# Later raw weights, one queue for the holes, and another order of block 0 in a fused RWKV-6 and tanh-shrink kernel

## The chip, the cores and the metric

One core of a Trainium2 chip runs the whole program in one launch. The metric is the device time of an execution in microseconds (us); runs are compared by their median.

## The reference, cut to what matters

Attention with a decaying state per head, for 4 batches, 8 heads, 768 tokens and 48 channels; then a dense block over 3072 tokens, 384 in, 2048 hidden, 384 out.

```python
for t in range(S):
    cur = np.einsum('bhd,bhe->bhde', u[None] * kt, vt)
    y[:, :, t] = np.einsum('bhd,bhde->bhe', rt, state + cur)
    state = wt[:, :, :, None] * state + np.einsum('bhd,bhe->bhde', kt, vt)
...
h = x @ w_in            # x: y as (3072, 384)
g = h - np.tanh(h)
return (g @ w_out).astype(np.float32)
```

## The kernel before

The work is cut into 8 blocks of 384 tokens (4 batches, two halves each). A block has an attention part and a dense part. While the dense part of block i runs, over 16 steps f of 128 hidden columns each, the attention of block i+1 is prepared between its steps. Block 0 has nobody before it: its attention is done by `boot`, alone, in two halves (pairs of heads 2 and 3, then 0 and 1).

**Attention.** Chunks of 64 tokens. `behind` (a scan on VectorE, L417) makes the decays behind each token, `take_whole` (L437) the whole decay of a chunk, `times_behind` (L431) multiplies k by them; `before` (L404, L405) and `times_before` (L424) do the same for r, into the tile `pre`. `own` and `earlier` are score products on TensorE (`gram`, L480), written through a mask by VectorE (L487). `turn` transposes k on TensorE (L502) and ScalarE copies it (L508). `update_half` (boot, L601) and `update_1` (L560) make the state products; the states are scans on VectorE in the boot (L616) and eleven small operations (L572) in block 0. `result` sums products with states (`from_states`, L662) and with scores (`from_scores`, L680); `result_out` (L714) copies the sum to the tiles `xT`. Rows for which there is no room go through the tile `late`, and `fill_holes` (L721) carries them by six small transfers of 24 KB into the holes of `xT`. In block 0 the term of a token with itself is made by `product_u`, `product_r`, `product_sum` (L370, L374, L378) from tokens loaded in another layout, and put in by `diagonal_in` (L385); the r tokens are loaded into the tile that `times_before` reads.

**Dense part.** Step f: `first` (L826) makes h on TensorE in a PSUM bank and ScalarE copies it out (L829). VectorE takes its square s (L855), ScalarE makes qa from s (L858), VectorE makes h times s and then g (twice L832). `Second.add` (L903) multiplies g with w_out, three steps later in block 0. Later blocks use a form with fewer products (L950). In block 0, h of step 0 and 3 onward goes to the bank `hp`, h of steps 1 and 2 to the first two banks of the sums, which `Second.add` needs after them.

**Weights.** They arrive as raw 64-bit words in 16 units of 768 KB (`more_weights`, L250), five buffers, in the order of `UNITS`. ScalarE converts a unit in three pieces (L263), VectorE joins them (L267). Three units are loaded and converted in the boot and right after; the others in block 0, so many pieces after step f as `PIECES` says.

**Order.** The instructions of TensorE, VectorE, ScalarE and SyncE (SP) stand in their queues in the order in which the program issues them; only GpSimd's (POOL) order is left to a scheduler. An engine waits at the head of its queue. `begin_behind(ins, dma)` makes a load wait until an instruction has ended; SP then holds everything behind it. `busy(to, n)` (L303) issues n products that nobody reads, beside the work. In `plan(0)`, `phases`, `before`, `ahead` and `loads` say behind which step f of block 0 a part of block 1 (or 2) is issued. `bound` (L448) is a sum on ScalarE that checks that no decay is over 1.

Of the kernel before, what the change touches and what calls it, by code (L numbers as in the profile page):

```python
# [52 lines left out]
L = 64  # L53
# [19 lines left out]
RAWS = 5  # L73
LAG = 2
LAST = 5
PIECES = 2, 1, 2, 3, 3, 3, 3, 3, 3, 3, 4, 4, 4
UNITS = [(0, 0), (0, 1)] + [u for j in range(NF // 2 - 2) for u in ((1, j), (0, j + 2))] + [(1, NF // 2 - 2),
                                                                                      (1, NF // 2 - 1)]
LATE = 3
# [46 lines left out]
def kernel(  # L126
# [181 lines left out]
    class Block:  # L308
# [153 lines left out]
        def gram(self, ps, lhs, rhs, p0, n, m=None, ahead=0, late=0):  # L462
            width = L // 2 if m else L
            ps_t = scratch(ps)
            busy(ps_t[:, 0], ahead)
            if late:
                busy(ps_t[:, 0], late, later_ident)
            used = ps_t[:, :, 0:n * NCP * width]
            gr = used.rearrange("s h (p c t) -> s h p c t", p=n, c=NCP)
            for p in range(p0, p0 + n):  # L470
                for c in range(NCP):
                    for h in range(2):
                        for par in range(2):
                            rows = slice(64 * h, 64 * h + D)
                            src = self.chunk(rhs, p, 2 * c + par, rhs == "pre" and not m)[rows]
                            dst = gr[64 * par:64 * par + 64, h, p - p0, c, :]
                            if m:
                                src = src.rearrange("d (b two m) -> d b two m", two=2, m=m)[:, :, 1, :]
                                dst = dst.rearrange("s (b m) -> s b m", m=m)
                            self.done = nc.tensor.matmul(dst, lhsT=self.chunk(lhs, p, 2 * c + par)[rows], rhs=src,  # L480
                                                         start=True, stop=True)
            return used

        def masked(self, ps, lhs, rhs, mask, p0, **fill):
# [102 lines left out]
        def update_half(self, pair, p0):  # L587

            self.by_column = [t[:, 0:D * NCH].rearrange("d (e c) -> d e c", c=NCH) for t in pair]
            for x in range(UP):  # L590
                if x:
                    nc.tensor.drain().then_inc(fence, 1)
                    fences.append(None)
                    nc.tensor.wait_ge(fence, len(fences))
                for c in range(0, NCH, 2):
                    for h in range(2):
                        for par in range(2):
                            p = (x + par) % UP
                            toks = slice(64 * par, 64 * par + 64)
                            e0 = (p0 + p) * D2 + h * D  # L600
                            nc.tensor.matmul(self.by_column[p][64 * h:64 * h + 64, :, (c + par + 1) % NCH],  # L601
                                             lhsT=self.ks[toks, p0 + p, c // 2, 64 * h:64 * h + 64],
                                             rhs=self.v[toks, c // 2, e0:e0 + D], start=True, stop=True)

# [64 lines left out]
        def from_scores(self, yp, slots, first, last):  # L669
            for n, slot in slots:  # L670
                for p in reversed(slot):
                    for c in range(NCP):
                        for h in range(2):
                            for par in range(2):
                                toks = slice(64 * par, 64 * par + 64)
                                e0 = 64 * (h ^ (p % 2))
                                f0 = p * D2 + h * D
                                n0 = (n * NCP + c) * L
                                wide = L if self.halved and p == KC - 1 else D
                                nc.tensor.matmul(yp[p % 2][e0:e0 + wide, par, n0:n0 + L],  # L680
                                                 lhsT=self.v[toks, c, f0:f0 + wide],
                                                 rhs=A[toks, h, p, c, :],
                                                 start=(first and n == slots[0][0] and c == 0),
                                                 stop=(last and (n, c) == (slots[-1][0], NCP - 1)),
                                                 skip_group_check=True)

        def results(self, ps, halved=False):
            self.width = D if halved or isinstance(ps, Kept) else L
# [315 lines left out]
    def plan(i):  # L1004
# [1 line left out]

        formed_w = {}
        if i == 0:
            phases = {5: ("turn",), 6: ("update",), 10: ("earlier",), 13: ("result 1",)}
            before = {0: ("behind 2", "take_whole 2"), 1: ("behind 0", "take_whole 0"), 2: ("times_behind 2",),  # L1010
                      3: ("times_behind 0",), 4: ("before 2",), 5: ("before 0",), 6: ("product_u", "bound 2"),
                      7: ("held", "bound 0"), 8: ("times_before",), 10: ("product_r",),
                      11: ("product_sum",), 12: ("diagonal_in 2", "diagonal_in 0")}
            ahead = {15: ("behind 2", "take_whole 2")}
            loads = {f: "weights" for f in (0, 1, 3, 4, 5, 6, 7, 8, 9, 10)}
# [51 lines left out]
    def run(ops):  # L1067
        for op in ops:
            op()
# [13 lines left out]
    def boot(ps, pair, blk, later):  # L1083
# [3 lines left out]
            blk.load(name, p0, n)  # L1087
        blk.load_v(h1, UP)
        blk.load("k", h2, UP)
        more_weights(nc.sync)  # L1090
        blk.load_v(h2, UP)
        blk.load("r", h2, UP)

# [10 lines left out]
        blk.turn_1(ps, h1)  # L1104
        blk.times_before(h1, UP)
        earlier = blk.earlier(ps, h1)
        begin_behind(blk.done, more_weights(nc.sync))
        blk.behind(h2, UP)
        blk.take_whole(h2, UP)
        first_a, first_b = convert(*raws.pop(0))  # L1110
        own()
        blk.turn_2(h1)
        run(first_a[:2])
        blk.update_half(pair, h1)
        blk.times_behind(h2, UP)
        blk.times_u(h2, UP)
        blk.turn_1(ps, h2)
        blk.turn_2(h2)
        earlier()
        run(first_a[2:])  # L1120
        blk.totals_by_column(h2)
        blk.results(ps, halved=True)
        blk.result("from_scores", both[0])
        run(blk.states_half(h1))
        blk.result("from_states", both[0], True)
        begin_behind(blk.opened, more_weights(nc.sync))
        blk.before(h2, UP)
        own = blk.own(ps, h2)
        blk.update_half(pair, h2)
        blk.times_before(h2, UP)  # L1130
        blk.result_out((3,), nc.scalar.copy)
        blk.result_out((2,))
        earlier = blk.earlier(ps, h2, ahead=2)
        blk.fill_holes([nc.sync, nc.gpsimd])
        begin_behind(blk.done, later.load("w"))
        more_weights(nc.sync)
        second_a, second_b = convert(*raws.pop(0))
        third_a, third_b = convert(*raws.pop(0))
        run(second_a)
        own()  # L1140
        onwards = blk.states_half(h2)
        blk.results(ps, halved=True)
        busy(blk.yp[0][:, 0], 4)
        blk.result("from_states", both[1])
        earlier(1, 1)
        earlier(0, 1)
        begin_behind(third_a[0](), more_weights(nc.sync))
        run(third_a[1:2])
        more_weights(nc.sync)
        later.load("k")  # L1150
        for p in reversed(both[1]):
            blk.result("from_scores", (p,), True, more=True)
        run(onwards)
        run(first_b)
        blk.result_out((1,), nc.scalar.copy)
        blk.result_out((0,), nc.vector.tensor_copy)
        run(third_a[2:])
        run(second_b)
        run(third_b)
        blk.held(0, NPAIR)  # L1160

    mains, pieces = ExitStack(), []
    ps_a = Kept(mains.enter_context(tc.tile_pool(name="ps_a", bufs=1, space=PSUM)))
    ps_h = mains.enter_context(tc.tile_pool(name="ps_h", bufs=1, space=PSUM))
    hp, *acc = [ps_h.tile([P, BANK], F32, name=name, tag=name) for name in ("hp", "acc0")]
    xT = blocks[0].begin()
    with tc.tile_pool(name="ps_boot", bufs=1, space=PSUM) as ps_boot:
        boot(Turns([scratch(ps_boot)] + ps_a.both), [hp] + acc, blocks[0], blocks[1])
# [24 lines left out]
    for i, blk in enumerate(blocks):  # L1193
# [8 lines left out]
        second = Second(row0, acc, few[i]) if few[i] < NF else None  # L1202
        for f in range(NF):
            now = i * NF + f
            for op in ahead_of_h:
                op()
            h, made = first(here, f, ([hp, *acc][f] if now in (1, 2) else hp)[:, 0:NB])
            g, ahead_of_h, square, later_ops = slight(h, now, i, f)
            some = ({4: (0, 2), 6: (2, 4), 8: (4, 6), 9: (6, 8), 14: (8, len(SUMS))} if later else
                    {4: (0, 4), 6: (4, 8), 8: (8, len(SUMS))}).get(f) if summed else None  # L1210
# [178 lines left out]
```

## Time and profile before

| what | value |
|---|---|
| median of 3 runs | 555.12 us (554.82 to 555.69) |
| the profiled execution | 555.16 us, its span 553.3 us |
| TensorE products, weight loads | busy 536.6 and 400.7 us |
| VectorE, ScalarE, GpSimd | busy 460.3, 404.3, 5.2 us |
| raw weights | 16 loads of 768 KB, median 5.3 us from issue to landing |
| HBM read, written | 44.73 MB, 4.72 MB |

PE is TensorE's products, PEld its weight loads, DVE is VectorE, ACT ScalarE, SPq the queue of SyncE. A row of a timeline has the start, the duration (of all that were merged), engine, line, operation, out<-in, shape and count, and in brackets the idle time before it with what ended it; "issue" means that the engine waited for nothing the profile shows. In a table of stretches the columns are the stretch, its length, the busy time of PE, PEld, DVE, ACT and POOL, the granted clock of TensorE, the busy share of the transfer engines and GB/s. A row of the queues has number of pieces, megabytes and share. L12 is line 12 of the kernel.

### The profile page before, as it was taken

To read this page: it belongs to the slowest core of one execution; us is meant where nothing else is said; L and a number is where in the kernel's file an instruction comes from. 1 tells how busy PE (TensorE), PEld (TensorE's weight loads), DVE (VectorE), ACT (ScalarE), POOL (GpSimd) and SP (SyncE) were. 2 spreads that over 40 slices of the span, in tenths; PEclk is the share of its full clock that TensorE was granted. 3 is DMA by queue.
4 is the path that set the end of the run, shared out by engine and by line. 5 is a ranking of instruction groups with operands and counts; after the bars stand their busy time and mean duration, and the time that the engine had idled before them with its cause. 6 is when DMAs were issued, how large, how long until landed. Compare 5 with 4: busy or idle time off the path is not lost.

```text
span 553.3 us, 13985 instructions
## 1 busy us (share of the span) xinstructions
PE 536.6 (97%) x5645; PEld 400.7 (72%) x5645; DVE 460.3 (83%) x942; ACT 404.3 (73%) x815; POOL 5.2 (1%) x33
## 2 busy tenths in 40 slices
PE   6789999999999999999999999999999999999996
PEld 3546566678777787778778787777878787787873
DVE  7699989999988899789797799979797897557563
ACT  5689897797667886588766886588865885666561
POOL 1100000000000000000000000000000000000000
PEclk9899999999999999999999999999999999999999
DMA  8598454243302642135211732136232420100101
GB/s 279 186 391 313 155 191 126 85 117 88 117 12 85 104 117 90 64 88 142 90 55 44 144 117 64 50 87 158 60 97 58 91 54 4 56 0 1 43 2 46
DMA packets 53445, 56.29 MB, mean 102 GB/s; under 512 B 21504, under 2 KB 51328, under 8 KB 53376
## 3 DMA queue, kind: packets, MB, share of 16 engines
q1 hardware_dynamic: 52992, 55.18, 33.9%
q8 instruction: 45, 0.74, 0.5%
q14 instruction: 24, 0.20, 0.1%
q10 hardware_dynamic: 288, 0.10, 0.1%
q0 software_dynamic: 96, 0.07, 0.0%
HBM read 44.73 MB, written 4.72 MB: 89 GB/s over the span
## 4 chain that ended last, share of the span: by engine, by line
PE 90%; ACT 2%; DVE 2%; issue 0%; PEld 0%; PEldq 0%; DVEq 0%
PE hp L826 43%; PE acc L950 26%; PE att L950 6%; PE acc L903 4%; PE att L680 2%; PE att L480 2%; PE att L662 2%; PE acc L928 2%; PE att L560 2%; ACT up L263 1%; DVE w_sb L267 0%; ACT h L829 0%; DVE s L855 0%; ACT qa L858 0%; DVE post L417 0%
## 5 line engine op out<-in xcount | busy, mean ns | idle before, releaser
L826 PE MATMUL hp<-xT,w_sb 128*128 128x384 f32 x756 | 265.9, 488 | 2.0 <-ACT h L829 1.9
L826 PEld LDWEIGHTS hp<-xT,w_sb 128*128 128x128 f32 x756 | 135.1, 190 | 74.6 <-ACT h L829 3.2
L829 ACT ACTIVATE h<-hp 128x384 f32<-128x384 f32 x126 | 61.6, 489 | 101.2 <-PE hp L826 101.1
L950 PE MATMUL acc<-forms,g 128*128 128x128 f32 x954 | 133.6, 276 | 0.5
L950 PEld LDWEIGHTS acc<-forms,g 128*128 128x128 f32 x954 | 121.6, 192 | 10.2 <-issue 1.2
L832 DVE SCALAR_TENSOR_TENSOR h<-h,s 128x384 f32<-128x384 f32 x128 | 70.7, 552 | 51.7 <-ACT s L847 51.6
L873 DVE TENSOR_TENSOR g<-g 128x256 f32<-128x256 f32 x265 | 103.4, 420 | 8.0 <-PE acc L950 7.2
L848 ACT ACTIVATE qa<-s,shift 128x384 f32<-128x384 f32 x113 | 69.6, 616 | 3.7
L850 ACT ACTIVATE junk<-s,shift 128x384 bf16<-128x384 f32 x113 | 67.7, 600 | 0.0
L832 DVE SCALAR_TENSOR_TENSOR g<-qa,h 128x384 f32<-128x384 f32 x112 | 61.7, 551 | 1.7 <-ACT qa L858 0.2
L847 ACT ACTIVATE s<-h 128x384 f32<-128x384 f32 x113 | 59.1, 523 | 3.6
L950 PEld LDWEIGHTS acc<-w_sb,g 128*128 128x128 f32 x318 | 46.7, 191 | 9.7 <-ACT sums L918 0.3
L950 PE MATMUL acc<-w_sb,g 128*128 128x128 f32 x318 | 53.1, 276 | 0.1
L950 PE MATMUL att<-w_sb,g 128*128 128x128 f32 x212 | 35.5, 275 | 0.0
L950 PEld LDWEIGHTS att<-w_sb,g 128*128 128x128 f32 x212 | 31.1, 192 | 5.3
L903 PE MATMUL acc<-w_sb,sums 128*128 128x384 f32 x96 | 34.1, 490 | 0.4 <-ACT h L829 0.3
L985 DVE TENSOR_TENSOR sums<-sums 128x256 f32<-128x256 f32 x84 | 33.0, 408 | 1.7 <-ACT sums L962 1.4
L263 ACT ACTIVATE up<-raw 128x768 f16<-128x768 f32 (+1 forms) x32 | 32.3, 1061 | 0.0
L903 PEld LDWEIGHTS acc<-w_sb,sums 128*128 128x128 f32 x96 | 17.8, 190 | 12.7 <-ACT h L829 0.9
L405 DVE TENSOR_TENSOR_SCAN pre<-w,start 128x780 f32<-128x780 f32 x14 | 25.0, 1783 | 0.5
L417 DVE TENSOR_TENSOR_SCAN post<-w,seed 128x780 f32<-128x780 f32 x14 | 24.9, 1776 | 0.0
L850 ACT ACTIVATION_READ_ACCUMULATOR junk<-s,shift 128x1 f32 x113 | 21.1, 187 | 0.0
(110 smaller groups left out, 513.4 us busy)
## 6 DMA issues: line engine op xcount, KB each, us to landing
raw<-in_weights SPq DMA_DIRECT2D x16, 768.0 KB, 5.3
w<-in_wT SPq DMA_DIRECT2D x7, 780.0 KB, 4.5
k<-in_kT SPq DMA_DIRECT2D x7, 768.0 KB, 4.7
r<-in_rT SPq DMA_DIRECT2D x7, 768.0 KB, 4.5
v_sb<-in_v SPq DMA_DIRECT2D x7, 576.0 KB, 4.0
k<-in_tokens SPq DMA_DIRECT2D x7, 576.0 KB, 3.9
r<-in_tokens SPq DMA_DIRECT2D x7, 576.0 KB, 5.2
out_y<-sums SPq DMA_DIRECT2D x18, 128.0 KB, 1.9
```

What stands on the lines that cost most here:

```text
L263: return lambda: nc.scalar.activation(out=to, in_=of, func=AF.Copy, scale=scale, bias=bias)
L405: return nc.vector.tensor_tensor_scan(out=self.tile("pre")[:, cols], data0=self.tile("w")[:, cols], data1=start[:, 0:n * NCH * LP], initia ...
L826: nc.tensor.matmul(hp, lhsT=w_in_sb[:, f, kc, :], rhs=xT[kc], start=(kc == KC - 1), stop=(kc == 0))
L829: return h, nc.scalar.activation(out=h, in_=hp, func=AF.Copy, scale=1.0 / UPSCALE)
L832: return lambda: nc.vector.scalar_tensor_tensor(out=out, in0=in0, scalar=scalar, in1=in1, op0=op0, op1=ALU.mult)
L847: nc.scalar.activation(out=s, in_=h, func=AF.Square)
L848: nc.scalar.activation(out=qa, in_=s, func=AF.Square, bias=shift[:, 4:5])
L850: nc.scalar.activation(out=junk[:, 0:NB], in_=s, func=AF.Relu, bias=shift[:, 5:6], accum_out=excess[:, at:at + 1])
L873: return lambda: nc.vector.tensor_tensor(out=G[:, to:to + 2], in0=two(G, g_at(q, a0), g_at(q, a1)), in1=two(G, g_at(q, b0), g_at(q, b1)), ...
L903: nc.tensor.matmul(acc, lhsT=g[:, j * P:(j + 1) * P], rhs=w_out_sb[:, f, :], start=(f == self.first), stop=(f == NF - 1))
L950: nc.tensor.matmul(to, lhsT=G[:, g_at(q, a), :], rhs=rhs, start=start, stop=stop, skip_group_check=True)
L985: ops.append(lambda op=op, at=at: nc.vector.tensor_tensor(out=at[0], in0=at[1], in1=at[2], op=OPS[op]))
```

## The change

- Raw weights of the boot: none is issued among the first loads. The first waits for the first product of `earlier` of half 1, the second for the last product of `from_scores` of half 1, the third for the last product of `update_half` of half 2; then `w` of block 1, a fourth without a gate, a fifth behind the second unit's last piece, k, and a sixth. The conversions move with them: in the boot two units whole and two pieces of the third (before: three units).
- Holes of the boot: all six transfers are issued by POOL (before: three by SP, three by POOL). One `busy` more, 5 for 4.
- `totals_by_column` of half 2 is issued earlier on ScalarE.
- Block 0: ScalarE's copy of h of a step stands ahead of qa of the step before (before: behind it). h of step 4 goes to a bank of `ps_a` instead of `hp`. Of the pieces of conversion, one follows step 0, three step 1, none the next two calls, then 2, 4, 3 and so on.
- Attention of block 1: `behind 2` with `take_whole 2` moves to the end of the boot; `behind 0` from step 1 to step 2; `times_behind`, `before`, `product_u`, `held`, `times_before`, `turn`, `update` each one step later; `bound` of block 1 from steps 6 and 7 to 9 and 10. `product_r`, `earlier` and what follows keep their steps.
- `bound` of block 0 moves from steps 13 and 14 of block 0 to steps 1 and 6 of block 1.

```diff
-PIECES = 2, 1, 2, 3, 3, 3, 3, 3, 3, 3, 4, 4, 4
+PIECES = 0, 0, 2, 4, 3, 3, 3, 3, 3, 3, 4, 4, 4
...
         if i == 0:
-            phases = {5: ("turn",), 6: ("update",), 10: ("earlier",), 13: ("result 1",)}
-            before = {0: ("behind 2", "take_whole 2"), 1: ("behind 0", "take_whole 0"), 2: ("times_behind 2",),
-                      3: ("times_behind 0",), 4: ("before 2",), 5: ("before 0",), 6: ("product_u", "bound 2"),
-                      7: ("held", "bound 0"), 8: ("times_before",), 10: ("product_r",),
+            phases = {6: ("turn",), 7: ("update",), 10: ("earlier",), 13: ("result 1",)}
+            before = {2: ("behind 0", "take_whole 0"), 3: ("times_behind 2",), 4: ("times_behind 0",),
+                      5: ("before 2",), 6: ("before 0",), 7: ("product_u",), 8: ("held",),
+                      9: ("times_before", "bound 2"), 10: ("product_r", "bound 0"),
                       11: ("product_sum",), 12: ("diagonal_in 2", "diagonal_in 0")}
...
         blk.load("k", h2, UP)
-        more_weights(nc.sync)
         blk.load_v(h2, UP)
...
-        begin_behind(blk.done, more_weights(nc.sync))
+        begin_behind(blk.opened, more_weights(nc.sync))
...
         blk.turn_2(h1)
-        run(first_a[:2])
+        blk.totals_by_column(h2)
         blk.update_half(pair, h1)
...
         earlier()
-        run(first_a[2:])
-        blk.totals_by_column(h2)
+        run(first_a[:2])
         blk.results(ps, halved=True)
         blk.result("from_scores", both[0])
+        begin_behind(blk.done, more_weights(nc.sync))
         run(blk.states_half(h1))
         blk.result("from_states", both[0], True)
-        begin_behind(blk.opened, more_weights(nc.sync))
...
         blk.update_half(pair, h2)
+        updated = blk.done
...
         earlier = blk.earlier(ps, h2, ahead=2)
-        blk.fill_holes([nc.sync, nc.gpsimd])
+        run(first_a[2:])
+        blk.fill_holes([nc.gpsimd])
+        begin_behind(updated, more_weights(nc.sync))
         begin_behind(blk.done, later.load("w"))
         more_weights(nc.sync)
...
-        run(second_a)
+        run(second_a[:2])
+        begin_behind(second_a[2](), more_weights(nc.sync))
...
-        busy(blk.yp[0][:, 0], 4)
+        busy(blk.yp[0][:, 0], 5)
...
-        begin_behind(third_a[0](), more_weights(nc.sync))
-        run(third_a[1:2])
+        later.load("k")
         more_weights(nc.sync)
-        later.load("k")
...
-        run(third_a[2:])
+        run(third_a[:2])
         run(second_b)
-        run(third_b)
+        later.prepare("behind 2")
+        later.prepare("take_whole 2")
         blk.held(0, NPAIR)
-
-    mains, pieces = ExitStack(), []
+        return [(third_a[2], third_b)]
...
-            for op in ahead_of_h:
+            for op in ahead_of_h if i else ():
                 op()
-            h, made = first(here, f, ([hp, *acc][f] if now in (1, 2) else hp)[:, 0:NB])
+            to = [hp, acc[0], acc[1], hp, ps_a.both[0][:, 0]][now] if now < 5 else hp
+            h, made = first(here, f, to[:, 0:NB])
+            for op in ahead_of_h if not i else ():
+                op()
...
-                ops = square + behind
+                ops = square + converting(pieces, 1)
             elif now == 1:
-                ops = rest + converting(pieces, 1) + square + formed + behind
+                ops = rest + square + converting(pieces, 3)
...
-            if i == 0 and f in (NF - 3, NF - 2):
-                blk.bound(HALVES[f - NF + 3])
-            if i == 0 and f == NF - 2:
+            if i == 1 and f in (1, 6):
+                blocks[0].bound(HALVES[f // 6])
+            if i == 1 and f == 6:
                 nc.gpsimd.memset(states[0][:, :, 0, 0:D], 0.0)
```

The rest of the diff keeps, in `gram`, `update_half` and `from_scores`, the first or the last product, for the gates.

More of the change, by code (lines that the diff above doesn't have):

```diff
@@ L464, in gram @@
             ps_t = scratch(ps)
+            self.opened = None
             busy(ps_t[:, 0], ahead)
@@ L481, in gram @@
                                                          start=True, stop=True)
+                            self.opened = self.opened or self.done
             return used
@@ L600, in update_half @@
                             e0 = (p0 + p) * D2 + h * D
-                            nc.tensor.matmul(self.by_column[p][64 * h:64 * h + 64, :, (c + par + 1) % NCH],
+                            self.done = nc.tensor.matmul(self.by_column[p][64 * h:64 * h + 64, :, (c + par + 1) % NCH],
                                              lhsT=self.ks[toks, p0 + p, c // 2, 64 * h:64 * h + 64],
@@ L679, in from_scores @@
                                 wide = L if self.halved and p == KC - 1 else D
[L680 to L685, printed above, removed]
+                                self.done = nc.tensor.matmul(yp[p % 2][e0:e0 + wide, par, n0:n0 + L],
+                                                             lhsT=self.v[toks, c, f0:f0 + wide],
+                                                             rhs=A[toks, h, p, c, :],
+                                                             start=(first and n == slots[0][0] and c == 0),
+                                                             stop=(last and (n, c) == (slots[-1][0], NCP - 1)),
+                                                             skip_group_check=True)
         def results(self, ps, halved=False):
@@ L1156, in boot @@
         blk.result_out((0,), nc.vector.tensor_copy)
-        run(third_a[2:])
+        run(third_a[:2])
         run(second_b)
-        run(third_b)
+        later.prepare("behind 2")
+        later.prepare("take_whole 2")
         blk.held(0, NPAIR)
-    mains, pieces = ExitStack(), []
+        return [(third_a[2], third_b)]
+    mains = ExitStack()
     ps_a = Kept(mains.enter_context(tc.tile_pool(name="ps_a", bufs=1, space=PSUM)))
@@ L1167 @@
     with tc.tile_pool(name="ps_boot", bufs=1, space=PSUM) as ps_boot:
-        boot(Turns([scratch(ps_boot)] + ps_a.both), [hp] + acc, blocks[0], blocks[1])
+        pieces = boot(Turns([scratch(ps_boot)] + ps_a.both), [hp] + acc, blocks[0], blocks[1])
     ps_d = mains.enter_context(tc.tile_pool(name="ps_d", bufs=1, space=PSUM))
```

## The prediction

> **What bounds the kernel now.** First the page: who is busy, at which clock, and what fetches code.
>
> ```profile
> PE 536.6 (97%) x5645; PEld 400.7 (72%) x5645; DVE 460.3 (83%) x942; ACT 404.3 (73%) x815; POOL 5.2 (1%) x33
> ...
> q8 instruction: 45, 0.74, 0.5%
> ```
>
> TensorE bounds the whole; only its idle time and its half-clock time can be won. Queue 8 is TensorE's code: 0.74 MB in 45 pieces is 16.4 KB each, and 11,290 loads and products over 45 is about 250 instructions a piece.
>
> Second, TensorE's waits up to 100 us and its timeline in the boot and at the `earlier` scores of block 1, with the DMA view of 19.4 to 19.6 and SP's timeline:
>
> ```profile
> PE hp L826 <- ACT h L829: 1.9, 1, 1.9
> ...
> 16.26 0.84 PE L662 MATMUL att<-pre,first_states 48*48 48x64 f32 x29 [0.55 <-issue]
> ...
> 21.70 0.25 PE L601 MATMUL acc<-v_sb,ks 64*64 64x48 f32 x1 [2.75 <-issue]
> ...
> q8 instruction: 1, 0.02, 29.2%
> ...
> 12.19 4.65 SPq L250 DMA_DIRECT2D raw<-in_weights  x2
> ```
>
> In the boot TensorE twice waits for nothing but "issue": until 16.26 and, for 2.75 us in the middle of `update_half`, until 21.70. I read both as waits for code: between the two resumes lie 126 loads, 126 products and 3 others, 255 instructions, one piece. A piece is asked for when the one before it is entered: the piece that ends the second wait was asked for at 16.26, and its transfer is the one at 19.40. It took 0.93, and TensorE resumed 1.36 later. Raw weights were issued at 16.50 (the second of the x2, ending at 16.84, 0.34 long), so the code waited 3.14 us behind them. The next piece, asked for at 21.70 with no raws under way, started after 1.12.
>
> Third, the engines in stretches, at the boot's end and in block 0:
>
> ```profile
> 23.00:24.00 1.00, 1.00 (x34) 0.61 (x23) 0.94 (x2) 0.62 (x1) 0.13 (x2) 0.60 0.00 0
> 24.00:25.00 1.00, 1.00 (x4) 0.17 (x2) 1.00 (x5) 0.00 (x0) 0.00 (x0) 0.50 0.37 42
> ...
> 40.00:46.00 6.00, 5.48 (x17) 3.34 (x18) 5.79 (x11) 6.00 (x10) 0.00 (x0) 1.00 0.92 336
> 46.00:52.00 6.00, 6.00 (x50) 3.84 (x52) 5.80 (x11) 6.00 (x10) 0.00 (x0) 1.00 0.92 321
> ```
>
> The column before the last two is the granted clock: 0.60, 0.50, 0.50, 0.70 in the four us from 23 is 3.4 us at half, after 3.4 us in which TensorE had run only 1.5. And VectorE (the third pair) works 5.8 of 6 us here: from 28 to 66 us it is as full as TensorE. What it must do before TensorE may go on decides. That place is here:
>
> ```profile
> 65.64 1.75 DVE L424 TENSOR_TENSOR pre<-r,pre 128x1536 f32<-128x1536 f32 x1
> ...
> 66.80 2.20 PE L826 MATMUL hp<-xT,w_sb 128*128 128x384 f32 x6
> ...
> 67.42 0.38 SPq L366 DMA_DIRECT2D r<-in_tokens  x1
> ...
> 68.94 1.63 PE L480 MATMUL att<-pre,post 48*64 48x64 f32 x96
> ...
> 73.66 1.36 DVE L374 TENSOR_TENSOR k<-k,r 128x1152 f32<-128x1152 f32 x1 [1.26 <-DMA r<-in_tokens]
> ```
>
> `times_before` (L424) ends at 67.39; the scores that need it (L480) start when their queue reaches them, at 68.94: VectorE is 1.5 us ahead. After 66.8 TensorE never waits again.
>
> **The change, part by part.** The sum is made against the profiled execution, 555.16 us (span 553.3), 0.04 over the median of 555.12.
>
> *Raws later.* No transfer is added; their places change. The first is now gated by the first product of `earlier` (11.2, so issued about 11.3), before the code piece asked for at 11.56 and so ahead of it; 11.3+2.9 (16.50 to 19.40) +0.93+1.36 gives 16.5 instead of 16.26. The second is gated by the last L680 (14.23+0.90) and issued at 15.2, 1.3 earlier than the raws of 16.50 before; the code behind it starts at 15.2+2.9=18.1 and TensorE resumes at 18.1+0.93+1.36=20.4 instead of 21.70. Then: rest of `update_half` 0.34, two fills 0.48 (7 took 1.68), L480 0.9, five fills 1.2 (one more than before, on the path: 0.24), L662 0.95, the fence 0.45 (as in the first half), L680 0.9: the L714 copies start at 25.6, at full clock, where they started at 28.02. Bounds: the next piece is asked for at 20.4 and the third raws are issued 0.40 later. Raws issued 0.24 after a request (16.26) held it up, those issued 0.63 after (11.56, 12.19) did not. If held, it starts at 20.8+2.9, TensorE resumes at 26.0 where it would be at 24.9, and the 2.4 us shrink to 1.3. I take 1.8, the middle, since 0.40 lies between the two rows.
>
> The Trainium skill (DMA: Bandwidth & Descriptors, Queues, rings and completion order) says an engine finishes a whole packet of descriptors of one queue before it turns to another; the 3.14 us agree.
>
> *Holes in POOL's queue alone.* Six issues at 0.52 (three took 1.57) from about 18.9 (18.31 before, plus the first raws landing later) end at 22.0; the last lands 3.1 later, at 25.1. The third part of the first L826 needs it at 26.9. Cost nothing, under 1.8 us of cover; SP's loads (w, raws) no longer stand behind them, but w waits for its own gate, L480.
>
> *h ahead of qa, and other banks.* The 1.9 us before L826 (waiting for h(3) behind a qa) and 0.8 us before L903 (for h(2)) go. They are worth nothing by themselves if VectorE is what TensorE meets next.
>
> *Scans and turn later.* From the end of VectorE's L714 copies on, its list up to L424 holds one step of the dense part more: L267, two L832, one L855, which take 67.31 to 69.82, 2.51 us. In the list the scan and its small op (1.92) stand before s(0), so s(0) ends 3.37 after the copies; then qa(0) 0.53 and three conversions on ScalarE (0.81+0.94+0.94) end at 6.6, while VectorE reaches their L267 at 5.9: a new wait of 0.8. One more for qa(7), 0.3. So L424 ends at 67.39+2.51+0.8+0.3-1.8=69.2, and L480 starts at 69.25 instead of 68.94: **+0.3**. The boot's gain is spent. TensorE arrives about 2.8 us earlier: it waits there. If the scan finds w late, this grows: w is issued at 22.2 behind 2 us of raws and took 4.7, so lands near 27; the scan is due at 29.14+0.87-1.8=28.2; cover 1 us.
>
> *r tokens.* Their load waits for L424; before, two dense steps and 1.26 of waiting lay between L424 and L374, now one. With the 6.2 us of before (67.42 to 73.6), L374 stays 6.2 behind L424, and the diagonal (L385, ended 84.94) comes at 84.94+3.6-1.8=86.75, against a slot for L680 at 86.10+0.3: +0.35. With the k tokens' 3.9 us nothing. The page's median for r tokens is 5.2: I take **+0.2**.
>
> *Bounds of w in block 1.* Two of 1.1 us on ScalarE, which waits for TensorE there (4.26 busy of 6 at 94 to 100). Nothing; a stall there would cost at most 2.2.
>
> *Clock.* A wait of 2.8 us fits into one 3.4 us stretch. The boot's stretch with 1.5 busy was followed by half clock; the wait before L826 left 1.6 busy in some 3.4 us and was not. With 0.6 to 1.9 busy, by phase, half clock follows in about three phases of five. It costs 3.4/2=1.7 if all dense; small products lose little (L662 32 in 0.72 at half, 22 in 0.42 at full, 17%), so with L480's 1.6 us inside it is 0.3+0.9=1.2. Bounds 0 and 1.7; I take **1.1**, near the second.
>
> The Trainium skill (TensorE: Matmul & The Clock Gate, Part 1) puts the drop after an idle window of about 3.4 us, free-running. By that a 2.8 us wait is harmless and the sum is 0.5; the trace had a drop after a window that was 44% busy, and the measurement decides.
>
> Sum: 0.3+0.2+1.1=+1.6: **556.8 us**.
>
> **The rivals.**
> - *No half clock*: the wait at L480 falls across two stretches. 555.7. Chance 0.25.
> - *Faster: the code passes the raws.* If the second piece starts 1.12 after its request, as at 21.70, TensorE resumes at 16.5+1.12+2.29=19.9, or 19.0 where the first piece is in time too; the copies come 2.9 to 3.8 us early, L480 at 68.2 to 67.2, 0.8 to 1.7 gained, with the clock kept. 553.9. Deciding point: the request must reach its engine before the raws of 15.2; the 16.26 row, lost with a lead of 0.24, speaks against. Chance 0.20.
> - *The third raws hold up the third piece*: 1.3 early instead of 1.8 and half clock, or in the boot once more: 557.5 to 558. Chance 0.12.
> - *The stall is no fetch* and stays at 21.70: only the boot's half clock is won, the copies come 1.1 early: 556.8+0.7=557.5. The Trainium skill (Runtime: NRT & Kernel Launch, Instruction fetch mechanics) calls fetching mostly hidden; 255 instructions between two resumes speak against it here. Chance 0.07.
>
> **The numbers.** 0.36 for the forecast. Faster by over 0.2% (1.1 us, about what a measurement of this kernel can tell): the second rival, 0.20. Slower: forecast, third, fourth, less a part near the bound: 0.53. Same: 0.27. Low 553.9 is the faster rival; high 558.0 the third.
>
> **What would show it.** After: an "issue" gap in `update_half` that ends near 20.4; L714 near 26; full clock at 24; then a wait of about 2.8 us of TensorE before the L480 of block 1 for L424, and half clock behind it. Wrong, if that wait is under 1 us, or L714 starts before 24.5.

## The result, and the profile after

The changed kernel takes 559.84 us (median of 7 runs, 557.3 to 561.71); the kernel before, run beside it on the same chip, takes 555.69 (554.59 to 555.98). The ratio is 1.0078, with a 95% interval of 1.0057 to 1.0099: slower by 0.8%. The profiled execution took 559.87 us (span 558.1), 4.71 more than the profiled execution before. Lines after L464 stand a few lines further down now: L480 is L481, L601 is L603, L662 is L664, L680 is L682, L714 is L716, L826 is L828, L903 is L905.

The page, its first line of busy time:

```profile
PE 540.1 (97%) x5646; PEld 403.4 (72%) x5646; DVE 460.5 (83%) x942; ACT 404.2 (72%) x815; POOL 6.7 (1%) x36
```

TensorE has one product more (the fifth fill, a product of `busy` that nobody reads) and is busy 3.5 us longer: nearly the same work ran longer at half clock. TensorE's waits up to 110 us, and its timeline in the boot:

```profile
PE att L481 <- DVE pre L424: 3.3, 1, 3.3
PE acc L603 <- issue: 3.0, 1, 3.0
...
PE hp L828 <- ACT h L831: 0.8, 1, 0.8
```

```profile
15.47 1.20 PE L664 MATMUL att<-pre,first_states 48*48 48x64 f32 x37 [0.31 <-PEq L704]
...
21.39 0.25 PE L603 MATMUL acc<-v_sb,ks 64*64 64x48 f32 x1 [3.03 <-issue]
...
23.20 2.32 PE L303 MATMUL att<-ident 128*128 128x512 bf16 x5
...
27.89 2.36 PE L828 MATMUL hp<-xT,w_sb 128*128 128x384 f32 x6
```

The first of the two code waits of before (until 16.26) is gone. The second is still there: TensorE arrives earlier and waits 3.03 us until 21.39, where it was 21.70. The five fills take 2.32 us, 0.46 each, so they ran at half clock, and the first dense product starts at 27.89 where it started at 27.87. In this execution the boot won 0.0 us, and that is the mildest case: in the profiles of e1, e3, e6, e9 and e12 below, which have the same boot up to there, the first dense product starts 0.76 to 1.73 us later than before, with two half-clock stretches in the boot.

The place that decides is the scores of block 1. TensorE's and VectorE's timelines, and the engines in stretches (in each row of these TensorE is the first pair, VectorE the third; the granted clock is the column before the last two):

```profile
65.51 2.10 PE L828 MATMUL hp<-xT,w_sb 128*128 128x384 f32 x6
70.92 2.84 PE L481 MATMUL att<-pre,post 48*64 48x64 f32 x96 [3.31 <-DVE pre L424]
73.69 4.04 PE L905 MATMUL acc<-w_sb,sums 128*128 128x384 f32 x6
```

```profile
35.96 0.96 DVE L267 SCALAR_TENSOR_TENSOR w_sb<-w_sb,up 128x768 int32<-128x768 int32 x1 [0.87 <-ACT up L263]
...
69.11 1.75 DVE L424 TENSOR_TENSOR pre<-r,pre 128x1536 f32<-128x1536 f32 x1
...
76.11 1.36 DVE L374 TENSOR_TENSOR k<-k,r 128x1152 f32<-128x1152 f32 x1 [2.74 <-DMA r<-in_tokens]
```

```profile
68.00:70.00 2.00, 0.00 (x0) 0.00 (x0) 1.87 (x5) 1.40 (x5) 0.00 (x0) 1.00 0.00 0
70.00:72.00 2.00, 1.08 (x40) 1.08 (x44) 2.00 (x3) 2.00 (x3) 0.00 (x0) 0.65 0.06 5
72.00:74.00 2.00, 2.00 (x69) 1.88 (x62) 1.24 (x4) 2.00 (x3) 0.13 (x2) 0.50 0.92 289
74.00:76.00 2.00, 2.00 (x4) 1.09 (x4) 0.00 (x0) 0.26 (x2) 0.00 (x0) 0.50 0.96 384
76.00:78.00 2.00, 2.00 (x5) 1.08 (x5) 1.89 (x2) 0.00 (x0) 0.00 (x0) 0.64 0.05 18
```

L424 starts 3.47 us later than before (69.11 against 65.64), after a new wait of VectorE for a conversion (until 35.96). TensorE stands still from 67.6 to 70.92, and then has its clock halved from 70.6 to 77.4, 6.83 us: two stretches of 3.41.

Where time is lost or won is best read from the starts of the dense part, one group of six L826 (L828) products in every step. The table gives these starts against the kernel before, all from the timelines, with the number of half-clock stretches (3.41 us each, the last of the run left out) in the clock records. It holds the experiments too, which are told below. Where the update (L562, 1.6 us) comes one step later, it lies between the columns 7 and 8 and not ahead of 7, so that column 7 looks 1.6 us better than it is; compare there from column 8 on. In e3 the scores come behind the start of step 11 and not ahead of it, which makes column 11 look 1.6 us better.

| kernel | step 0 | 4 | 7 | 8 | 10 | 11 | 14 | half stretches |
|---|---|---|---|---|---|---|---|---|
| before, us | 27.87 | 40.52 | 54.96 | 58.83 | 66.80 | 72.53 | 87.59 | 1 (boot) |
| changed | +0.02 | -2.70 | -2.85 | -1.06 | -1.29 | +5.04 | +5.04 | 1 boot, 2 at the scores |
| e1 | +1.59 | -1.13 | +4.25 | +4.25 | +4.02 | +3.92 | +4.52 | 2 boot, 1 at step 6 |
| e2 | -0.21 | -0.23 | -1.64 | -0.22 | -0.45 | +3.25 | +3.25 | 2 boot, 1 at the scores |
| e3 | +1.35 | -1.37 | -1.50 | +0.28 | +0.05 | -1.81 | +7.68 | 2 boot, 2 at the results |
| e4 | -1.70 | -3.12 | -3.32 | -1.54 | -1.77 | +4.55 | +4.55 | 1 boot, 2 at the scores |
| e5 | -0.40 | -3.11 | -1.25 | -1.25 | -1.48 | -1.59 | -1.59 | 1 boot |
| e6 | +0.76 | -1.96 | -2.07 | -0.29 | -0.52 | +2.74 | +2.74 | 2 boot |
| e7 | -3.27 | -1.80 | -1.80 | -1.80 | -1.82 | -1.82 | -1.82 | 0 |
| e8 | -3.42 | -1.85 | -2.80 | -1.19 | -1.42 | +4.90 | +4.90 | 1 behind step 3, 2 at the scores |
| e9 | +1.65 | -1.06 | -1.15 | +0.63 | +0.40 | +1.14 | +2.29 | 2 boot |
| e12 | +1.73 | +3.13 | +3.14 | +3.14 | +3.12 | +3.12 | +3.12 | 2 boot |
| e10 | -3.38 | -6.10 | -4.04 | -4.04 | -4.27 | -4.38 | -4.38 | 0 |
| e11 | -3.41 | -5.35 | -5.24 | -3.72 | -3.95 | -2.79 | -2.56 | 0 |

In the changed kernel TensorE is 1.29 us ahead when step 10 begins and 5.04 behind when step 11 does; from there to the last block nothing moves by more than 0.1. The whole loss lies between two rows: 1.98 us at the start of the scores (70.92 against 68.94) and 3.06 us of half clock behind it. The number of half stretches in one kernel varies from run to run (among the 7 runs one, at 557.3 us, had a mean clock of 0.996, that of before, where the profiled one has 0.988), so a median and a profile can differ by a stretch or two. The ratios below come from all runs of a kernel, the table from one profile of each.

### The profile page after: what moved, and what is told of

Read it like the earlier page. It is cut to its first block, busy times and chain, and to the rows that moved or that the text cites. A ratio compares the mean times of both kernels' runs of the same rounds, so it can differ in the third digit from the quotient of the medians.

```text
span 558.1 us, 13997 instructions
## 1 busy us (share of the span) xinstructions
PE 540.1 (97%) x5646; PEld 403.4 (72%) x5646; DVE 460.5 (83%) x942; ACT 404.2 (72%) x815; POOL 6.7 (1%) x36
## 4 chain that ended last, share of the span: by engine, by line
PE 87%; DVE 8%; issue 2%; PEld 1%; ACT 1%; DMA 0%; PEldq 0%; DVEq 0%; SPq 0%
PE hp L828 41%; PE acc L952 26%; PE att L952 6%; PE acc L905 4%; PE att L481 2%; PE att L682 2%; PE att L664 2%; PE acc L930 2%; PE att L562 1%; DVE w_sb L267 1%; DVE post L417 1%; DVE pre L405 1%; DVE states L574 1%; DVE s L857 1%; DVE h L834 1%
## 5 line engine op out<-in xcount | busy, mean ns | idle before, releaser
L828 PE MATMUL hp<-xT,w_sb 128*128 128x384 f32 x750 | 263.7, 488 | 0.8 <-ACT h L831 0.8
L828 PEld LDWEIGHTS hp<-xT,w_sb 128*128 128x128 f32 x750 | 134.4, 191 | 72.3 <-ACT h L831 1.4
L905 PE MATMUL acc<-w_sb,sums 128*128 128x384 f32 x96 | 35.8, 512 | 0.1
L905 PEld LDWEIGHTS acc<-w_sb,sums 128*128 128x128 f32 x96 | 18.6, 199 | 13.1 <-issue 1.5
```

The source lines that it names most:

```text
L828: nc.tensor.matmul(hp, lhsT=w_in_sb[:, f, kc, :], rhs=xT[kc], start=(kc == KC - 1), stop=(kc == 0))
L905: nc.tensor.matmul(acc, lhsT=g[:, j * P:(j + 1) * P], rhs=w_out_sb[:, f, :], start=(f == self.first), stop=(f == NF - 1))
```

## The experiments

Theory A is that VectorE's later L424, and the clock behind TensorE's wait for it, make the loss, while the boot wins nothing because the code still comes behind raws. The rivals are the boot itself (B), h first with its banks and the moved pieces (C), and the r tokens with the bounds (D).

**e1: the steps of block 1 back.** In the changed kernel:

```
-            phases = {6: ("turn",), 7: ("update",), ...
-            before = {2: ("behind 0", ...), 3: ..., 8: ("held",), 9: ("times_before", "bound 2"), ...
+            phases = {5: ("turn",), 6: ("update",), ...
+            before = {1: ("behind 0", ...), 2: ..., 7: ("held",), 8: ("times_before",), 9: ("bound 2",), ...
```

> The changed kernel, with block 1's turn, update, totals, scans and times_before back at the dense steps where they stood before (behind 2 stays at the boot's end); all other edits kept. Theory A (the loss is VectorE's one dense step more ahead of L424, TensorE's 3.3 us wait for it and the half clock behind it): L424 ends 2.5 us earlier, at 68.35, TensorE waits under 1 us at L481, no half clock behind it, 554.5 to 555.3. Theory B (the boot's raws and fills lose the time): TensorE's queue stays late, 559 or more. Theory C (h ahead of qa, the other banks and the pieces lose it): 558 to 560 as well, with waits in block 0 that stay. Theory D (r tokens and bounds in block 1): 559 less about 1.

Measured: 559.0 us, ratio 1.0045 (1.0024 to 1.0067). A's number was missed. The wait at L481 did go, but another came ahead of it, at the update:

```profile
PE att L562 <- ACT ks L510: 1.6, 1, 1.6
```

and half clock behind that (55.4 to 58.9). With the steps back, TensorE comes to the update before ScalarE, whose queue of conversions is full, has copied ks. In the changed kernel the later update covers this; it only passes the wait on. The experiment changed two places at once, so it could not decide; e9 does.

**e2: the later steps alone**, in the kernel before:

```
-            phases = {5: ("turn",), 6: ("update",), ...
-            before = {..., 1: ("behind 0", ...), 2: ("times_behind 2",), ... 8: ("times_before",), ...
+            phases = {6: ("turn",), 7: ("update",), ...
+            before = {..., 2: ("behind 0", ...), 3: ("times_behind 2",), ... 9: ("times_before",), ...
```

> The kernel before, with nothing changed but turn, update, scans, totals and times_before of block 1 one dense step later (behind 2 stays at step 0). Theory A: L424 ends one step (2.5 us) later, at 69.9; TensorE arrives at 68.9 and waits 1.0, L480 at 70.0; 556.2 without half clock, up to 558 with one or two stretches of it. Theories B, C and D: the steps alone cost nothing, 555.2 to 555.5.

Measured: 558.85 us, ratio 1.0062 (1.0040 to 1.0084). A's upper end, 558, was passed too. B, C and D said 555.2 to 555.5 and are out as sole causes: this one edit has most of the loss. Its profile:

```profile
70.64 2.70 PE L480 MATMUL att<-pre,post 48*64 48x64 f32 x96 [2.19 <-DVE pre L424]
73.27 2.68 PE L903 MATMUL acc<-w_sb,sums 128*128 128x384 f32 x6
```

The scores start 1.70 late, and one half stretch follows: +3.25 at step 11.

**e3: the scores one step later** in TensorE's order, in the changed kernel: `10: ("earlier",)` becomes `11: ("earlier",)`.

> The changed kernel, with the scores of block 1 that wait for L424 one dense step later in TensorE's order (phase earlier at 11 instead of 10): nothing on VectorE or ScalarE changes ahead of it. Theory A: TensorE has some 3.5 us of dense products to run ahead of the scores, arrives when L424 is done, waits under 0.5, no half clock: 555.2 to 556. Theories B and C (TensorE's own queue is late by then): 558.5 to 560.

Measured: 562.51 us, ratio 1.0119 (1.0098 to 1.0141). The wait for L424 went as A said, and step 11 came 1.81 early (1.6 of it because the scores now lie behind), but the time was missed by 7 us. The wait moved to the results, and grew:

```profile
86.75 0.45 PE L664 MATMUL att<-pre,states 48*48 48x64 f32 x4 [4.05 <-DVE scores L489]
```

The masks (L489, 85.69) now stand in VectorE's list behind L374, which waited 3.42 us for the r tokens, whose load waits for L424. So the r tokens, unseen in the changed kernel's total, are the next wait in line. Two half stretches followed here too.

**e4: the second raws behind the code**, in the changed kernel's boot:

```
-        begin_behind(blk.done, more_weights(nc.sync))
         run(blk.states_half(h1))
...
         own = blk.own(ps, h2)
+        begin_behind(blk.done, more_weights(nc.sync))
```

> The changed kernel, with the second raws of the boot gated by the last product of own (17.3) instead of the last L682 (15.2). Theory A, on the boot: the code piece asked for at 15.6 starts ahead of the raws, near 16.7, the stall in update_half shrinks from 3.0 us to about 0.7 and ends near 19.1, no half clock in the boot, the L716 copies start at 25 to 26.5 (the holes that land at 25.1 may hold the first L828 then). The wait at L481 stays 3.3, since VectorE and TensorE both start earlier: 559.8 less 1.5 to 3.1, 556.7 to 558.3. Rival (the stall is no code behind raws): it stays at 21.4 and the time at 559.8.

Measured: 559.36 us, ratio 1.0061 (1.0034 to 1.0088). The mechanism is shown: the code piece starts at 16.49 instead of 18.98 (queue 8), the stall is 0.56 us and ends at 18.72, the copies start 3.52 earlier. The time is not:

```profile
18.72 0.25 PE L603 MATMUL acc<-v_sb,ks 64*64 64x48 f32 x1 [0.56 <-issue]
...
26.17 3.65 PE L828 MATMUL hp<-xT,w_sb 128*128 128x384 f32 x6 [1.72 <-DMA xT<-late]
```

```profile
24.52 1.12 DVE L716 COPY xT<-att 48x384 f32<-48x384 f32 x2 [1.50 <-PE att L682]
27.97 1.78 DVE L417 TENSOR_TENSOR_SCAN post<-w,seed 128x780 f32<-128x780 f32 x1 [1.33 <-DMA w<-in_wT]
...
35.48 0.96 DVE L267 SCALAR_TENSOR_TENSOR w_sb<-w_sb,up 128x768 int32<-128x768 int32 x1 [1.58 <-ACT up L263]
```

TensorE waits for the holes and runs the first group at half clock; VectorE waits for w and twice for conversions. L424 starts at 68.64, 0.47 earlier than in the changed kernel. Of 3.5 us won in the boot, 0.5 reach the scores.

**e5: h first alone**, in the kernel before: h is made and evicted ahead of the qa of the step before, in the banks of the change.

> The kernel before, with nothing changed but h ahead of qa in block 0 and the banks of the first five h. Theory A: TensorE's 1.9 and 0.3 us waits for h go, it comes 2 us earlier to the scores, finds L424 at 67.4 and waits some 0.5 to 1 us: L480 at 67.5 instead of 68.9, 553.7; with a stretch of half clock behind that wait, 555.4. Theory C (h first costs time, since ScalarE's qa, conversions and ks copies come later): TensorE waits at L560 for the ks copies, 557 to 559.

Measured: 554.42 us, ratio 0.9990 (0.9970 to 1.0009), not to be told from 1. In the profile it wins 1.59: the waits for h go (step 4 at -3.11), and 1.6 us come back at L560 for the ks copies. That wait is the one that C named; C's loss is not there.

**e6: the wait filled.** In the changed kernel, 13 idle products ahead of the scores of block 1:

```
-                return [getattr(self, name)(ps, p0) for p0 in HALVES]
+                fill = {"ahead": 13} if name == "earlier" and self is blocks[1] else {}
+                return [getattr(self, name)(ps, p0, **(fill if p0 == HALVES[0] else {})) for p0 in HALVES]
```

> The changed kernel, with 13 idle products (128x512, 0.24 us each, 3.1 us) in TensorE's queue ahead of the scores of block 1, into the bank that they fill: the wait for L424 is filled with work and not shortened. Theory A: L481 starts at 70.9 as before, no half clock behind it, 2.0 us later than the kernel before: 556.8 to 557.4. Rival (the 3 us that follow the wait are lost to something else, such as code or operands that come late): 559.5 to 560.

Measured: 557.96 us, ratio 1.0040 (1.0023 to 1.0058), 0.6 above A's range; 557.46 in the profiled run. The same stretches as above:

```profile
68.00:70.00 2.00, 2.00 (x11) 0.84 (x9) 1.87 (x6) 1.46 (x4) 0.00 (x0) 1.00 0.31 122
70.00:72.00 2.00, 1.51 (x26) 0.67 (x28) 2.00 (x2) 1.96 (x3) 0.00 (x0) 1.00 0.00 0
72.00:74.00 2.00, 2.00 (x94) 1.67 (x84) 1.87 (x4) 2.00 (x3) 0.13 (x2) 1.00 0.49 121
```

Full clock throughout, with 3.0 us of useless products in place of idleness. The step from 10 to 11 costs 3.26 more than before, where it cost 6.33 more in the changed kernel: the clock is 3.1 us of the loss, and here the filled wait was cheaper than the same wait left empty. (This run had a second half stretch in the boot, +0.76.)

**e7: the second raws behind the code, in the kernel before.** The gate moves from the first L662 (`blk.opened`) to the last product of `own`, as in e4.

> The kernel before, with nothing changed but the gate of the boot's second raws: the last product of own (17.9) instead of the first L662 (16.3). Theory A: the code piece asked for at 16.26 starts ahead of the raws, the stall in update_half ends near 19.5 instead of 21.70, the L714 copies start 2 us earlier, VectorE's list up to L424 and TensorE's queue both come earlier by that: 552.8 to 553.8. Rivals: the half clock of the boot only moves to the first dense step, where it costs 1.7 us, 554.5 to 555.2; or the raws that come later hold up ScalarE's conversions and with them VectorE, 555 to 556.

Measured: 553.49 us, ratio 0.9966 (0.9948 to 0.9984), within A's range. The stall is shorter and ends at 19.51:

```profile
19.51 0.25 PE L601 MATMUL acc<-v_sb,ks 64*64 64x48 f32 x1 [1.11 <-issue]
```

There is no half clock anywhere ahead of the end, step 0 comes 3.27 early, and 1.82 of that is left at step 11: two waits for h, 2.0 and 1.8 (1.9 and 0.3 before), take the rest. Here the holes stand in two queues, and eight conversions are done before the copies (six in e4). So less hangs on the raws that follow; that part of the gain lasts for this reason is a reading and was not tried by itself.

**e8: the boot in order**, in the changed kernel: e4, holes in two queues, and w (gated by `updated`) ahead of the raws.

> The changed kernel with the second raws behind the code piece, as in e4, and with the holes in two queues again and the loads of w ahead of the raws that follow them. Theory A: L716 copies at 24.5, no wait for holes at the first L828 (1.7 us in e4) and none for w at L417 (1.3 us in e4): L424 ends 2.5 to 3.3 us earlier, with the same wait of TensorE and half clock behind it, 556.5 to 557.3. Rival (the holes land late because the DMA engines are full, in whichever queue they stand): 558.5 to 559.5, as e4.

Measured: 560.34 us, ratio 1.0080 (1.0051 to 1.0110). A failed. No holes were waited for, but ScalarE waited in front of a conversion, and h behind it in its queue:

```profile
ACT w_sb L263 <- DMA raw<-in_weights: 3.1, 1, 3.1
```

L424 starts at 68.94, 0.17 earlier than in the changed kernel, with a boot that ended 3.4 us earlier. The time lies above the rival's range too. With six conversions done before the copies (eight before the change) and the raws later, block 0's start here hung on the raws, not on the boot's end.

**e9: L424 alone back**, in the changed kernel: `8: ("held", "times_before"), 9: ("bound 2",)`. Turn, update and scans stay late.

> The changed kernel, with times_before (L424) alone back at dense step 8: turn, update and scans stay one step later. Theory A (only the place of L424 in VectorE's list decides): L424 ends near 68.3 instead of 70.9, TensorE waits under 1 us at L481, no half clock there: 559.8 less 2.5 and less 2 to 3 of half clock, 554.5 to 556. Rival (the later turn, update and scans themselves lose the time): 558 to 560, the loss at the update or the results instead.

Measured: 556.45 us, ratio 1.0012 (0.9998 to 1.0026), a little above the range; the boot had a second half stretch in the profiled run (+1.65). At the place in question:

```profile
70.07 1.63 PE L481 MATMUL att<-pre,post 48*64 48x64 f32 x96 [0.77 <-DVE pre L424]
71.63 2.20 PE L905 MATMUL acc<-w_sb,sums 128*128 128x384 f32 x6
```

The wait is 0.77 instead of 3.31, no half clock follows, and the step from 10 to 11 costs 0.74 more than before instead of 6.33 (by step 14 another 1.15 is lost, 0.62 of it in two short waits for h). Against the changed kernel's ratio of 1.0078 this one op, one step earlier, takes back 0.7%. The load of the r tokens, which waits for it, moves with it, but in the changed kernel that load was not on the path. That the later turn, update and scans lose the time by themselves is out.

**e12: the boot of the change alone**, in the kernel before; plan, h and pieces of block 0 as before.

> The kernel before with the boot of the change alone (raws later, holes in POOL's queue, first_totals and pieces reordered, five fills, k of block 1 ahead of a raw); plan, h and pieces of block 0 as before. Theory A: the code still comes behind raws, the stall ends near 21.4, half clock again at 23 to 26 or a stretch more: 554.8 to 556.5, no gain. Theory of the prediction's sum: 553.4. Rival (the boot is what loses the change's time): 558 to 559.5.

Measured: 558.0 us, ratio 1.0039 (1.0022 to 1.0056). It is above what A expected and at the lower end of the rival's 558 to 559.5: the boot is no zero by itself but loses 0.4%. The stall ends late again, at 22.01, two half stretches follow (+1.73), and VectorE and TensorE wait 1.3 and 1.4 for ScalarE's conversions and h in the first steps (+3.13 at step 4).

```profile
PE acc L905 <- ACT h L831: 1.4, 1, 1.4
```

The 553.4 of the prediction's sum is out by 4.6. The losses of e2 (0.6%) and e12 (0.4%) do not simply add up to the changed kernel's 0.8%, as h first, which is part of the change, wins some of it back: with L424 back (e9) everything else in the change together costs 0.1%.

**e10: code first and h first together**, in the kernel before: the edits of e5 and e7.

> The kernel before with two edits: the boot's second raws gated by the last product of own (e7), and h ahead of qa with its banks (e5). Theory A: in e7 TensorE gave 1.5 of its 3.3 us back in two waits for h (2.0 and 1.8); with h first they go, and TensorE meets the ks copies at L560 as in e5 (some 1.6): 552.0 to 553.2, without half clock. Rival (the wait for ks now has half clock behind it, or the raws that come later hold up h in ScalarE's queue): 553.5 to 555.5.

Measured: 552.22 us, ratio 0.9939 (0.9920 to 0.9958), within A's range. It beats both kernels. Its scores start 4.38 earlier and wait for nothing:

```profile
19.41 0.25 PE L601 MATMUL acc<-v_sb,ks 64*64 64x48 f32 x1 [1.11 <-issue]
...
47.32 1.63 PE L560 MATMUL att<-v_sb,ks 64*48 64x48 f32 x80 [1.60 <-ACT ks L508]
...
64.56 1.63 PE L480 MATMUL att<-pre,post 48*64 48x64 f32 x96
```

The edits seem to help each other: e7 gave 1.5 of its gain back at h, e5 could not be told from no change, and 0.34% and 0.10% became 0.61%, though the intervals are too wide to show that it is more than the sum.

**e11: e10 with the update one step later** (phase 7).

> The kernel of e10 with the update of block 1 (L560 and its L572) one dense step later (phase 7), turn and all else in place. Theory A: the ks copies are done when TensorE reaches L560, and L572's 6 us of VectorE come behind more of the list, so L424 ends earlier still; TensorE runs ahead until it meets the scores or the results: 550.5 to 552.5. Rival: L572 then lies ahead of the masks and the results, which TensorE waits for with half clock behind it: 554 to 557.

Measured: 552.53 us, ratio 0.9938 (0.9918 to 0.9957): no gain over e10. The wait for ks goes, and 1.2 us at the scores for L424 and 1.3 for h take its place. L424 starts at 64.34, later than in e10 (62.43), where A expected it earlier: ScalarE waited 1.6 us for raws, and the start of block 0 slid again.

## Why the prediction was wrong

The direction was right, and the place, and for the reason given: a wait for L424 and half clock behind it. The size was 1.6 us where 4.7 were measured, and 559.84 lies above the highest time that was allowed for, 558.0. Of the signs that were named, the wait (3.31) and the half clock behind it came; the stall ended at 21.39 and not near 20.4, the copies (L716) started at 28.04 and not near 26, and the clock at 24 was half and not full. By its steps:

- *Raws later: 1.8 us early.* Wrong; 0.0, and up to 1.7 late in other profiles with this boot. The first piece came in time (L664 runs unbroken from 15.47), so TensorE asked for the second at about 15.5, not 16.5, and still behind the raws issued at 15.24. Its transfer then started 3.74 us after those raws, not 2.9, and TensorE resumed 1.47 after its end: 18.98+0.93+1.47 = 21.4, not 20.4. The sum also had the rest of the boot at full clock; with 1.43 us of work in the 3.41 us stretch that ended at 22.8, as before (1.49), half clock came again, and the fills and L664 ran in it. In e4, where these raws are issued behind the request, the same piece started 2.49 earlier. The Trainium skill (DMA: Bandwidth & Descriptors, Queues, rings and completion order), by which an engine drains a whole packet of one queue before it turns to another, agrees with that. The third raws did no harm: issued at 21.78, 0.39 after the next request, they did not hold up its piece, which started at 22.50; that rival is out.
- *What the boot's gain is worth.* The step that moved VectorE's whole list earlier by the boot's gain would have failed too: e4 and e8 won 3.5 us before the copies and L424 came 0.5 and 0.2 earlier, held by w, holes and raws. It was taken for a shift of the list; the data did not shift with it. In e7 and e10, with eight conversions done before the copies, 1.8 of 3.3 and 3.2 of 3.4 us reached L424.
- *Holes:* no wait in the changed kernel, as said, but only since the boot won nothing; at e4's start they cost 1.72.
- *h first: nothing.* Right for the changed kernel: it is 1.06 ahead at step 8 and 1.29 at step 10, all of it spent in the wait for VectorE's L424. In e10, with VectorE earlier, it counts.
- *Scans and turn: L424 ends at 69.2.* Right once the 1.8 is taken out: 71.0, measured 70.86. One dense step more (2.51) and a new wait for the conversions (0.87 at 35.96, predicted 0.8) make up nearly all of the 3.47. The wait at L481 was 3.31, predicted 2.8.
- *r tokens: +0.2.* Not on the path: L374 waited 2.74 for them, but L385 ended 1.9 before the slot of its L682, which had moved by 5. e3 showed what they cost when the rest is not late.
- *Bounds in block 1: nothing.* Right: from step 11 on the distance to before stays at 5.0.
- *Half clock: 1.1, at most 1.7.* The mechanism was right, the size off: 3.06, as two stretches followed the wait. The bound assumed that one stretch of half clock follows and that small products lose little in it (17%, from L662 in the boot), 0.3 for the scores and 0.9 for the dense work. The 96 score products took 2.84 where they take 1.63 at full clock, which is 1.21 lost and not 0.3; the six L905 behind them, all at half clock, took 4.04 where they took 2.20, which is 1.84 and not 0.9. The first half stretch held the wait's last 0.3 us and then small products, and was followed by another. e6 shows that the clock is the cause of this term; why the second stretch follows is read from many profiles (below) and was not tried by itself. The rival "no half clock" is out in this kernel: the wait fell nearly whole into one stretch (67.20 to 70.61), which held 0.41 us of work.

So the two failed steps are the boot's gain of 1.8, which was 0.0 and so turned the +0.3 at the scores into +2.0, and the clock's 1.1, which was 3.06. The rival "stall stays at 21.70" came nearest to what the boot did, for another reason than it gave; "faster" would have needed the request ahead of the raws, which is what e7 arranged.

## What to carry to other kernels

When two engines are both nearly full, a moved step is priced at the place where one next waits for the other: here one vector op that stood one step later cost 0.7% and all the rest of the change together 0.1%, and moving only it back took nearly the whole loss away, though it made no gain (e9, 1.0012). A gain at the start of a chain counts only if the loads behind it come earlier too, so follow each load that is due in the next few us. And a wait of TensorE can cost itself plus the clock behind it (3.3 and 3.1 us here): move the work so that it doesn't arise (e9), or, second best, fill it with idle products (e6).

## What the runs showed of the hardware

The clock changes in stretches of 3.41 us whose phase differs from run to run. TensorE's busy time was worked out for each stretch up to 92 us from its rows, in all fourteen profiles. Seventeen stretches at full clock with 0.1 to 1.92 us of work were followed by half clock (1.92 in e2, 1.85 in e4), those with 2.0 or more never. But thirteen with 1.47 to 1.98 us kept the clock: five of nearly all dense 128x384 products, 1.47 to 1.85 us (one each in before, e5 and e12, two in e7), and eight at the start of the boot, 1.68 to 1.98 us, nearly all fills of 128x512. One of the dense kind in e8 (1.75) did not. A half stretch was followed by another where it held waits or small products and was not full (2.2 to 3.2 us, ten of them), and by full clock where it was full, or held dense products (e4, 2.99; e3, 3.32). So it looks as if the kind of work counts and not its time alone; no run settled what is counted, and no threshold comes out of these rows. The Trainium skill (TensorE: Matmul & The Clock Gate, Part 1) names a stretch of 3.4 us, free-running, which the records show, and a drop after an idle stretch: here stretches that were up to 56% busy (1.92 of 3.41 us) were followed by it too, and the measurement decides.

TensorE's code was the other surprise. One 16 KB piece held up behind loads of the same kernel (asked for at 16.26, started at 19.40 in the kernel before, at 17.19 in e7) stalled TensorE there, with half clock behind the stall in the kernel before and none in e7, and to issue one load 1.1 us later (e7) won 0.3% of the whole time. The Trainium skill (Runtime: NRT & Kernel Launch, Instruction fetch mechanics) calls the crossing from one block of code to the next mostly hidden. Here 255 loads and products ran in some 2.7 us (16.26 to 18.95 in the kernel before), and it was not hidden: TensorE stood 2.75 us.
